# Mask products one step later, and a new order of loads, transposes and mask build, in a block-sparse attention with a feed-forward layer

## The chip, the cores and the metric

The kernel runs on one core of a Trainium2 chip. The metric is the device time of one execution in microseconds (us). An execution is called slow when it is more than 1.5% above the fastest of its kernel. Ratios and intervals leave those executions out; the quoted medians of four still contain them.

The engines: TensorE (PE) multiplies matrices, VectorE (DVE) and ScalarE (ACT) work element by element, GpSimd (POOL) does the same and issues most loads here, and SyncE (SP) issues the stores and the DMA transposes.

## The reference

Four batches, 8 heads, 768 positions, head size 64. A 768x768 mask in blocks of 32 says which keys a query sees. The attention output, as 3072 tokens of 512 values, goes through an RMS norm and a gated feed-forward layer.

```python
scores = scale * np.matmul(q, k.transpose(0, 1, 3, 2))
mask = ...                       # neighbours, first and last block, 3 sampled blocks per row
scores = np.where(mask, scores, -1e9)
attn = softmax(scores); attn_out = np.matmul(attn, v)
x = attn_out.transpose(0, 2, 1, 3).reshape(B * S, H * D)      # 3072 x 512
xn = x / sqrt(mean(x * x) + 1e-6) * rms_g
g = xn @ w_gate                                               # 512 -> 1536
out = (g * sigmoid(g) * (xn @ w_val)) @ w_out                 # 1536 -> 512
```

## The kernel before

The work is cut into 8 units: a unit `u` is one batch and one half of its queries (384 columns). Attention of a unit takes 12 steps: 4 head pairs `pr` with 3 steps each. A step computes two of the six key tiles `jt`: scores on TensorE (`qk_mm`), exp on ScalarE (`exp_`), mask product on VectorE (`mask_`). The sum over keys (`av`, `zsum`) and the normalisation (`norm_a` to `norm_e`) follow. The feed-forward (FF) items of the preceding units are fed in between by a credit scheme, so that TensorE has work while exp and mask run. The schedule is written out by hand: instructions stand in each engine's queue in the order in which the program emits them.

```python
def load_pair(b, pr):                       # q and k of one head pair: 4 loads
    ...                                     # tile layout (c, h, d) inside the pair
    for t, src in ((qraw[b], qv), (kraw[b], kv)):
        ...
        for h in range(2):
            nc.gpsimd.dma_start(out=dst[:, h], in_=sp[:, h])

def transposes_dma(b, pr):                  # 2 transposes per head pair
    x = qkpool.tile([P, 2, S], BF16, name="qkT", tag="qkT")
    for i, src in enumerate((qraw[b], kraw[b])):
        nc.sync.dma_start_transpose(
            out=x[:, i, :].rearrange("q (c p) -> q c p", c=NC),
            in_=src[:, 2 * pr:2 * pr + 2, :].rearrange("p h w -> p (h w)"))

def mask_build(ic):                         # one half of the mask, six evictions on VectorE
    qm = ...matmul...; nc.vector.tensor_copy(out=Qvis[:, cols], in_=qm)
    for jt in range(NC):
        mp = ...matmul...
        nc.vector.tensor_copy(out=Mk[:, jt, cols], in_=mp)

def av(n, shared):
    ...                                     # 12 matmuls into o_
    nc.scalar.copy(out=osb[u][:, pr, :], in_=o_)
    nc.gpsimd.tensor_tensor(                # the squares o2 for the norm
        out=o2s[u][:, pr, :], in0=osb[u][:, pr, :], in1=osb[u][:, pr, :], op=ALU.mult)

def norm_a(u): ...                          # zw += o2 (matmul), zs = copy of zw
def norm_b(u): ...; nc.gpsimd.tensor_tensor(out=rs, in0=ms, in1=nhalf, op=ALU.pow)   # the power
def norm_c(u): ...; nc.vector.tensor_tensor(out=fx, in0=rz, in1=rs..., op=ALU.mult)

# FF item g:  gp = wg.T @ xn;  th = tanh(gp/2) on ScalarE;  uu = (th+1)*gp on VectorE
# FF item v:  vp = wv.T @ xn;  hp = uu * vp on VectorE
# FF item y:  yp += hp.T @ wo; copy on ScalarE, store

LAG = 8
for n in range(NU * NP):
    s1 = 3 * (n + 1)
    at(s1, 1.2, av, n, n >= 8); at(s1, 0.7, zsum, n)
    if pr == NP - 1: ...                    # norm_a at s1 + 1 ... norm_e at s1 + 5 and s1 + 7
at(2, 1.6, mask_build, 1)
for b in range(1, B):
    for pr in range(NP):
        at(3 * (8 * (b - 1) + pr) + 1, 0, load_pair, b, pr)
        at(3 * (8 * (b - 1) + pr + (3 if b == 1 else 2)) + 1, 0, transposes_dma, b, pr)
    at(3 * (8 * (b - 1) + (1 if b == 1 else 4)) + 1, 0, load_v, b)
at(4, 0, load_wo)
# FF of unit u starts at step 12 * (u + 1) + LAG

# one step
sa = qk_mm(n, 2 * j);      exp_(n, 2 * j, sa)
sb = qk_mm(n, 2 * j + 1)
if step == 0: ...                           # mask_build(0) here
else:
    if queue: since += feed()               # one FF item
    exp_(n, 2 * j + 1, sb)
    mask_(n, 2 * j); mask_(n, 2 * j + 1)    # behind the exp of their own step
... # then the fixed work of the step, then more FF items by credit
```

The softmax here doesn't subtract the row's maximum and nothing guards it: scores larger than these inputs give would overflow.

## Time and profile before

| | before |
|---|---|
| time, median of the first 3 runs | 394.03 us (391.96 to 394.90) |
| span of the profiled run | 390.7 us |
| TensorE / VectorE / ScalarE busy | 85% / 64% / 57% |
| first FF matmul | 73.65 us |
| one unit in the steady state | 42.34 us |

The page's busy times, and its row of the granted TensorE clock in 40 slices of the span (tenths of full speed), of the kernel before:

```profile
PE 332.0 (85%) x2426; PEld 157.2 (40%) x2454; DVE 249.2 (64%) x527; ACT 222.1 (57%) x353; POOL 93.4 (24%) x130
...
PE   2687508798879999998989898999899899999995
...
PEclk9969756999989999999999999999999999999999
```

One slice is 9.8 us. The zero in the sixth place of the TensorE row belongs to a hole from 44.8 to 58.7 us. A caution on the clock row: its first nines are not a measurement. The trace's clock entries begin only at about 17 us here, and the time before them is counted as full speed; yet the 12 transposes of one tensor took 0.85 us at 15.03 us and 0.50 us at 27.11 us.

TensorE's waits, longest in total first (who waited for whom: total us, times, longest us):

```profile
PE zw L312 <- POOL o_324 L293: 13.9, 1, 13.9
PE vp L411 <- DVE hp L414: 5.4, 11, 0.9
...
PE mp L203 <- DVE Qvis L199: 2.6, 2, 2.0
```

The first line is the hole: one single wait of 13.9 us, in which the normalisation of unit 0 waits for a square (o2) on GpSimd. The timeline of GpSimd shows why it came late (start us, us, engine, line, operation, and in brackets the idle time before it and what ended that):

```profile
43.72 1.69 POOL L83 DMA_DIRECT2D qb<-in_q_dram  x2
47.33 0.82 POOL L83 DMA_DIRECT2D kb<-in_k_dram  x1 [1.92 <-DMA vb<-in_v_dram]
57.01 0.82 POOL L83 DMA_DIRECT2D kb<-in_k_dram  x1 [8.86 <-DMA wo<-in_moe_w_out_dram]
57.84 0.84 POOL L293 TENSOR_TENSOR o_324<-osb 128x384 bf16<-128x384 f32 x1
```

A load issue sat at the head of GpSimd's queue until the wo load had landed, and the square stood behind it. The chain of waits has the same story in three lines (start us, us, what):

```profile
37.72 19.00 DMA wo<-in_moe_w_out_dram
...
57.84 0.85 POOL o_324 L293
58.69 0.04 issue
58.73 0.48 PE zw L312
```

In the steady state, the busy times of one unit (window from one unit's power on GpSimd to the next: length, busy us of each engine, granted clock, DMA share, GB/s), and VectorE's waits in the same stretch:

```profile
221.23:263.57 42.34, 39.02 (x289) 18.46 (x293) 29.14 (x63) 27.55 (x45) 4.18 (x6) 1.00 0.10 29
```

```profile
DVE uu L400 <- ACT th L398: 6.1, 6, 2.7
DVE pt L268 <- ACT pt L262: 4.8, 5, 1.5
DVE hp L414 <- PE vp L411: 1.2, 3, 0.4
```

TensorE's waits in the same stretch:

```profile
PE vp L411 <- DVE hp L414: 1.1, 2, 0.9
PE yp L425 <- issue: 0.6, 4, 0.2
...
PE gp L394 <- DVE uu L400: 0.5, 1, 0.5
```

TensorE's records lack 3.3 us of being full. Of these, 0.6 us stand before yp matmuls where records are missing (the trace has 32 of the unit's 36), so some 2.7 us are really idle. VectorE is busy only 29.14 us, but for 4.8 us it stands before a mask product whose exp is not ready.

### The profile page before, as it was taken

To read this page: it belongs to the slowest core of one execution; us is meant where nothing else is said; L and a number is where in the kernel's file an instruction comes from. 1 tells how busy PE (TensorE), PEld (TensorE's weight loads), DVE (VectorE), ACT (ScalarE), POOL (GpSimd) and SP (SyncE) were. 2 spreads that over 40 slices of the span, in tenths; PEclk is the share of its full clock that TensorE was granted. 3 is DMA by queue.
4 is the path that set the end of the run, shared out by engine and by line. 5 is a ranking of instruction groups with operands and counts; after the bars stand their busy time and mean duration, and the time that the engine had idled before them with its cause. 6 is when DMAs were issued, how large, how long until landed. Compare 5 with 4: busy or idle time off the path is not lost.

```text
span 390.7 us, 6305 instructions
## 1 busy us (share of the span) xinstructions
PE 332.0 (85%) x2426; PEld 157.2 (40%) x2454; DVE 249.2 (64%) x527; ACT 222.1 (57%) x353; POOL 93.4 (24%) x130
## 2 busy tenths in 40 slices
PE   2687508798879999998989898999899899999995
PEld 1223103344334444444444443444444444555552
DVE  4866406767856776567765876667756777666550
ACT  1448406686747676676666566756667667333331
POOL 8934712115444110044334100001000101000000
PEclk9969756999989999999999999999999999999999
DMA  5999999008866930053999520000000000000012
GB/s 72 184 211 180 170 183 134 3 0 81 81 42 41 143 74 2 27 59 33 90 107 107 82 67 29 27 3 27 3 27 29 29 0 29 27 29 28 27 48 88
DMA packets 70850, 25.58 MB, mean 65 GB/s; under 512 B 58020, under 2 KB 67748, under 8 KB 70820
## 3 DMA queue, kind: packets, MB, share of 16 engines
q0 software_dynamic: 47600, 14.16, 35.0%
q1 hardware_dynamic: 23220, 11.02, 12.2%
q8 instruction: 19, 0.31, 0.3%
q14 instruction: 11, 0.09, 0.1%
HBM read 28.31 MB, written 6.29 MB: 89 GB/s over the span
## 4 chain that ended last, share of the span: by engine, by line
PE 50%; DVE 19%; ACT 11%; DMA 10%; issue 4%; POOL 4%; POOLq 0%; DVEq 0%; ACTq 0%
PE gp L394 10%; PE yp L425 10%; PE vp L411 9%; ACT pt L262 7%; DVE pt L268 7%; DMA wo<-in_moe_w_out_dram 5%; DMA wv<-in_moe_w_val_dram 5%; DVE uu L400 5%; PE zw L303 4%; ACT th L398 3%; DVE xn L379 3%; DVE hp L414 3%; PE oa L287 1%; PE vw L411 1%; PE gw L394 1%
## 5 line engine op out<-in xcount | busy, mean ns | idle before, releaser
L268 DVE TENSOR_TENSOR pt<-pt,Mk 128x768 bf16<-128x768 bf16 x192 | 101.9, 558 | 38.6 <-ACT pt L262 34.9
L400 DVE SCALAR_TENSOR_TENSOR uu<-th,gp 128x384 bf16<-128x384 bf16 x90 | 49.7, 552 | 50.2 <-ACT th L398 50.0
L411 PE MATMUL vp<-xn,wv 128*128 128x384 bf16 x360 | 74.0, 328 | 5.9 <-DVE hp L414 5.4
L394 PE MATMUL gp<-xn,wg 128*128 128x384 bf16 x360 | 73.9, 328 | 5.5 <-DVE uu L400 4.3
L398 ACT ACTIVATE th<-gp 128x384 bf16<-128x384 f32 x90 | 44.3, 492 | 52.9 <-PE gp L394 50.3
L425 PE MATMUL yp<-wo,hp 128*128 128x512 bf16 x260 | 70.8, 381 | 3.5 <-issue 3.1
L414 DVE TENSOR_TENSOR hp<-uu,vp 128x384 bf16<-128x384 bf16 x90 | 49.7, 552 | 14.1 <-PE vp L411 9.2
L394 PEld LDWEIGHTS <-wg 128*128 128x128 bf16 x384 | 35.6, 98 | 41.3 <-issue 16.7
L411 PEld LDWEIGHTS <-wv 128*128 128x128 bf16 x384 | 36.0, 99 | 35.3 <-issue 14.5
L255 PEld LDWEIGHTS <-qkT 64*128 64x128 bf16 x384 | 14.0, 95 | 65.4 <-issue 60.9
L425 PEld LDWEIGHTS <-hp 128*128 128x128 bf16 x288 | 26.2, 99 | 28.7 <-issue 7.5
L287 PEld LDWEIGHTS <-vb 128*64 128x64 bf16 x384 | 21.4, 114 | 18.0 <-issue 11.0
L83 POOL DMA_DIRECT2D kb<-in_k_dram x24 | 19.6, 819 | 16.3 <-DMA wo<-in_moe_w_out_dram 8.9
L431 ACT ACTIVATE yo<-yp 128x512 f32<-128x512 f32 x24 | 14.3, 597 | 15.3 <-PE yp L425 13.6
L303 PE MATMUL zw<-pt,Ez 128*32 128x384 bf16 x384 | 22.6, 344 | 0.0
L83 POOL DMA_DIRECT2D qb<-in_q_dram x24 | 20.5, 856 | 1.9 <-DMA wv<-in_moe_w_val_dram 1.9
L338 POOL TENSOR_TENSOR rs<-ms,nhalf 128x3 f32<-128x3 f32 x8 | 7.1, 887 | 44.4 <-DVE ms L335 44.4
L379 DVE SCALAR_TENSOR_TENSOR xn<-osb,gcol,fb 128x384 bf16<-128x384 f32 x28 | 15.9, 608 | 0.0
L312 PE MATMUL zw<-o_324,Ew 128*32 128x384 bf16 x4 | 0.8, 372 | 13.9 <-POOL o_324 L293 13.9
L303 PEld LDWEIGHTS <-Ez 128*32 128x32 bf16 x384 | 7.5, 98 | 12.6 <-issue 11.0
L316 DVE COPY zs<-zw 128x384 f32<-128x384 f32 x8 | 4.4, 551 | 12.7 <-PE zw L312 12.7
L287 PE MATMUL oa<-pt,vb 128*64 128x384 bf16 x96 | 12.2, 404 | 0.0
(558 smaller groups left out, 422.1 us busy)
## 6 DMA issues: line engine op xcount, KB each, us to landing
out_dram<-yo SPq DMA_DIRECT2D x24, 256.0 KB, 2.0
vb<-in_v_dram POOLq DMA_DIRECT2D x4, 768.0 KB, 8.1
qb<-in_q_dram POOLq DMA_DIRECT2D x24, 96.0 KB, 3.6
kb<-in_k_dram POOLq DMA_DIRECT2D x24, 96.0 KB, 3.7
wg<-in_moe_w_gate_dram POOLq DMA_DIRECT2D x2, 768.0 KB, 12.5
wv<-in_moe_w_val_dram POOLq DMA_DIRECT2D x2, 768.0 KB, 16.1
wo<-in_moe_w_out_dram POOLq DMA_DIRECT2D x1, 1536.0 KB, 19.0
qb<-in_q_dram POOLq DMA_DIRECT2D x2, 192.0 KB, 3.5
```

What stands on the lines that cost most here:

```text
L83: nc.gpsimd.dma_start(out=dst[:, h], in_=sp[:, h])
L262: nc.scalar.activation(out=ptiles[n][:, jt, :, :], in_=s_[:, :, 0:TG], func=AF.Exp, scale=SCALE)
L268: nc.vector.tensor_tensor(out=pv, in0=pv, in1=Mk[:, jt, ic * TG:(ic + 1) * TG].unsqueeze(1).to_broadcast([P, 2, TG]), op=ALU.mult)
L287: nc.tensor.matmul(out=o_[64 * e:64 * e + 64, :], lhsT=vb[:, 2 * pr + e, jt * D:(jt + 1) * D], rhs=pt_[:, jt, e, :], start=(jt == 0), stop ...
L303: nc.tensor.matmul(out=zwt[u][32 * c:32 * c + 32, :], lhsT=Ez[:, pr, :], rhs=pt_[:, 2 * j2 + par, e, :], start=(pr == 0 and j2 == 0), stop ...
L379: nc.vector.scalar_tensor_tensor(out=xns[u][:, pr, :], in0=osb[u][:, pr, :], scalar=gcol[:, pr:pr + 1], in1=fb[i], op0=ALU.mult, op1=ALU.mult)
L394: nc.tensor.matmul(out=gp, lhsT=wg[:, c, f * P:(f + 1) * P], rhs=xns[u][:, c, :], start=(c == 0), stop=(c == NP - 1))
L398: nc.scalar.activation(out=th, in_=gp, func=AF.Tanh, scale=0.5)
L400: nc.vector.scalar_tensor_tensor(out=uu, in0=th, scalar=1.0, in1=gp, op0=ALU.add, op1=ALU.mult)
L411: nc.tensor.matmul(out=vp, lhsT=wv[:, c, f * P:(f + 1) * P], rhs=xns[u][:, c, :], start=(c == 0), stop=(c == NP - 1))
L414: nc.vector.tensor_tensor(out=hps[u][:, f, :], in0=uu, in1=vp, op=ALU.mult)
L425: nc.tensor.matmul(out=yp, lhsT=hps[u][:, f, t * P:(t + 1) * P], rhs=wo[:, f, :], start=(f == 0), stop=(f == NF - 1))
```

## The change

Its intent: give VectorE mask products whose exp has long been done, take the first normalisation off GpSimd's load queue, put batch 1's loads in an order in which nothing needed soon stands behind a large load, make one DMA transpose per tensor and batch, build the mask in pieces and start the FF of unit 0 a step earlier.

```diff
-    def load_pair(b, pr): ...
+    def load_c(b, i, c):                     # rows (c, head, d): one load per tensor and c
+        nc.gpsimd.dma_start(
+            out=flat[:, c * DM:(c + 1) * DM].rearrange("p (h d) -> p h d", h=H),
+            in_=src[b, :, :, c * D:(c + 1) * D])
...
-    def transposes_dma(b, pr): ...           # 2 per head pair
+    def transposes_dma(b, i):
+        nc.sync.dma_start_transpose(
+            out=qk[b][:, i].rearrange("q c r p -> q (c r) p"),
+            in_=(qraw, kraw)[i][b].rearrange("p h w -> p (h w)"))
...
-        nc.gpsimd.tensor_tensor(
+        (nc.vector if u == 0 else nc.gpsimd).tensor_tensor(
             out=o2s[u][:, pr, :], in0=osb[u][:, pr, :], in1=osb[u][:, pr, :], op=ALU.mult)
...
-    LAG = 8
+    LAG = 9
-        at(s1, 1.2, av, n, n >= 8)
-        at(s1, 0.7, zsum, n)
+        at(s1 + 1, 1.25, av, n, n >= 8)
+        at(s1 + 1, 0.7, zsum, n)
... # normalisation one step later; unit 0's second half of norm_e at s1 + 6
-    at(2, 1.6, mask_build, 1)
+    at(1, 0.3, mask_query, 0); at(1, 0.3, mask_build, 0, 0, 4); at(2, 0.3, mask_build, 0, 4, 6)
+    at(5, 0.3, mask_query, 1)
+    for i in range(3):
+        at(6 + i, 0.3, mask_build, 1, 2 * i, 2 * i + 2)
...
+                at(base + (7 + c if b == 1 else 1 + 2 * c + i), 0, load_c, b, i, c)
+            at(base + 17, 0, transposes_dma, b, i)
-    at(4, 0, load_wo)
+    at(13, 0, load_wo)
...
-    START = UST + LAG
+    starts = [UST + 7] + [UST * (u + 1) + LAG for u in range(1, NU + 1)]
...
+                for m in late:
+                    mask_(*m)                # the two products of the step before
+                late = [(n, 2 * j), (n, 2 * j + 1)]
                 if queue:
                     since += feed()
                 exp_(n, 2 * j + 1, sb)
-                mask_(n, 2 * j)
-                mask_(n, 2 * j + 1)
```

(Cut: the layout of the transposed tile, TensorE's transposes of batch 0 with one copy on ScalarE, and one load each for wg and wv in place of two.)

More of the change, by code (lines that the diff above doesn't have):

```diff
@@ L49 @@
     vpool = ctx.enter_context(tc.tile_pool(name="vpool", bufs=2))
-    qkpool = ctx.enter_context(tc.tile_pool(name="qkpool", bufs=8))
+    qkpool = ctx.enter_context(tc.tile_pool(name="qkpool", bufs=2))
     ppool = ctx.enter_context(tc.tile_pool(name="ppool", bufs=2))
@@ L71, in load_qk @@
         nc.gpsimd.dma_start(out=kraw[b][:, lo:hi, :], in_=kv[b, :, lo:hi, :])
-    def load_pair(b, pr):
-        if b not in qraw:
-            qraw[b] = raw.tile([P, H, NC * D], BF16, name="qb", tag="qb")
-            kraw[b] = raw.tile([P, H, NC * D], BF16, name="kb", tag="kb")
-        for t, src in ((qraw[b], qv), (kraw[b], kv)):
-            dst = t[:, 2 * pr:2 * pr + 2, :].rearrange("p h w -> p (h w)").rearrange(
-                "p (c h d) -> p h c d", c=NC, h=2)
-            sp = src[b, :, 2 * pr:2 * pr + 2, :].rearrange("p h (c d) -> p h c d", c=NC)
-            for h in range(2):
-                nc.gpsimd.dma_start(out=dst[:, h], in_=sp[:, h])
+    def load_c(b, i, c):
+        src, t = ((qv, qraw), (kv, kraw))[i]
+        if b not in t:
+            t[b] = raw.tile([P, H, NC * D], BF16, name="qb", tag=("qb", "kb")[i])
+        flat = t[b].rearrange("p h w -> p (h w)")
+        nc.gpsimd.dma_start(
+            out=flat[:, c * DM:(c + 1) * DM].rearrange("p (h d) -> p h d", h=H),
+            in_=src[b, :, :, c * D:(c + 1) * D])
     def load_v(b):
@@ L137, with load_w @@
     wvv = moe_w_val.rearrange("(c p) f -> p c f", p=P)
-    FH = DFF // 2
-    def load_w(i):
-        nc.gpsimd.dma_start(out=wg[:, :, i * FH:(i + 1) * FH], in_=wgv[:, :, i * FH:(i + 1) * FH])
-        nc.gpsimd.dma_start(out=wv[:, :, i * FH:(i + 1) * FH], in_=wvv[:, :, i * FH:(i + 1) * FH])
+    def load_w():
+        nc.gpsimd.dma_start(out=wg, in_=wgv)
+        nc.gpsimd.dma_start(out=wv, in_=wvv)
     def load_wo():
@@ L159, with transposes @@
     qk = {}
-    def transposes(b, pr, early=False):
-        x = qkpool.tile([P, 2, S], BF16, name="qkT", tag="qkT")
-        qk[(b, pr)] = x
-        if early:
-            tt = [ps_f.tile([P, 1024], BF16, name="tq", tag="gp"),
-                  ps_f.tile([P, 1024], BF16, name="tk", tag="vp")]
-        else:
-            t_ = ps_s.tile([P, 2, 1024], BF16, name="tqk", tag="s")
-            tt = [t_[:, 0, :], t_[:, 1, :]]
+    def transposes(b, pr):
+        if b not in qk:
+            qk[b] = qkpool.tile([P, 2, NC, NP, P], BF16, name="qkT", tag="qkT")
+        x = qk[b][:, :, :, pr, :]
+        tt = [ps_f.tile([P, 1024], BF16, name="tq", tag="gp"),
+              ps_f.tile([P, 1024], BF16, name="tk", tag="vp")]
         for i, src in enumerate((qraw[b], kraw[b])):
@@ L175, in transposes, with mask_query @@
                         in_=src[:, 2 * pr + h, c * D:(c + 1) * D], identity=ident)
-        if early:
-            for i in range(2):
-                nc.vector.tensor_copy(out=x[:, i, :], in_=tt[i][:, 0:S])
-        else:
-            nc.vector.tensor_copy(out=x, in_=t_[:, :, 0:S])
-    def transposes_dma(b, pr):
-        x = qkpool.tile([P, 2, S], BF16, name="qkT", tag="qkT")
-        qk[(b, pr)] = x
-        for i, src in enumerate((qraw[b], kraw[b])):
-            nc.sync.dma_start_transpose(
-                out=x[:, i, :].rearrange("q (c p) -> q c p", c=NC),
-                in_=src[:, 2 * pr:2 * pr + 2, :].rearrange("p h w -> p (h w)"))
+        for i in range(2):
+            (nc.scalar.copy if i == 1 and pr == 0 else nc.vector.tensor_copy)(
+                out=x[:, i], in_=tt[i][:, 0:S].rearrange("q (c p) -> q c p", c=NC))
+    def transposes_dma(b, i):
+        if b not in qk:
+            qk[b] = qkpool.tile([P, 2, NC, NP, P], BF16, name="qkT", tag="qkT")
+        nc.sync.dma_start_transpose(
+            out=qk[b][:, i].rearrange("q c r p -> q (c r) p"),
+            in_=(qraw, kraw)[i][b].rearrange("p h w -> p (h w)"))
     Qvis = const.tile([32, S], BF16, name="Qvis")
     Mk = const.tile([P, NC, S], BF16, name="Mk")
-    def mask_build(ic):
+    def mask_query(ic):
         cols = slice(ic * TG, (ic + 1) * TG)
-        qm = ps_a.tile([32, TG], FP32, name="qm", tag="zw")
+        qm = ps_a.tile([32, TG], FP32, name="qm", tag="acc")
         nc.tensor.matmul(
@@ L199, in mask_build @@
         nc.vector.tensor_copy(out=Qvis[:, cols], in_=qm)
-        for jt in range(NC):
+    def mask_build(ic, lo, hi):
+        cols = slice(ic * TG, (ic + 1) * TG)
+        for jt in range(lo, hi):
             mp = (ps_a.tile([P, TG], FP32, name="mp", tag="acc") if jt % 2
@@ L241 @@
     nc.gpsimd.memset(nhalf, -0.5)
-    load_w(0)
-    load_w(1)
+    load_w()
     ptiles, osb, zwt, xns, hps, o2s = {}, {}, {}, {}, {}, {}
@@ L252, in qk_mm @@
         s_ = ps_s.tile([P, 2, 512], FP32, name="s_", tag="s")
-        x = qk[(b, pr)]
+        x = qk[b]
         for e in range(2):
@@ L256, in qk_mm @@
                 out=s_[:, e, 0:TG],
-                lhsT=x[64 * e:64 * e + 64, 1, jt * P:(jt + 1) * P],
-                rhs=x[64 * e:64 * e + 64, 0, ic * TG:(ic + 1) * TG], start=True, stop=True)
+                lhsT=x[64 * e:64 * e + 64, 1, jt, pr, :],
+                rhs=x[64 * e:64 * e + 64, 0, ic * NT:(ic + 1) * NT, pr, :],
+                start=True, stop=True)
         return s_
@@ L447 @@
         s1 = 3 * (n + 1)
-        at(s1, 1.2, av, n, n >= 8)
-        at(s1, 0.7, zsum, n)
+        at(s1 + 1, 1.25, av, n, n >= 8)
+        at(s1 + 1, 0.7, zsum, n)
         if pr == NP - 1:
-            at(s1 + 1, 0.4, norm_a, u)
-            at(s1 + 2, 0.5, norm_b, u)
-            at(s1 + 3, 0.0, norm_c, u)
-            at(s1 + 4, 0.3, norm_d, u)
-            at(s1 + 5, 0.35, norm_e, u, 0)
-            at(s1 + 7, 0.35, norm_e, u, 1)
-    for pr in range(1, NP):
-        at(3 * (pr - 1) + 1, 0.95, transposes, 0, pr, True)
-    at(2, 1.6, mask_build, 1)
-    for b in range(1, B):
-        for pr in range(NP):
-            at(3 * (8 * (b - 1) + pr) + 1, 0, load_pair, b, pr)
-            at(3 * (8 * (b - 1) + pr + (3 if b == 1 else 2)) + 1, 0, transposes_dma, b, pr)
-        at(3 * (8 * (b - 1) + (1 if b == 1 else 4)) + 1, 0, load_v, b)
-    at(4, 0, load_wo)
+            when = (2, 3, 4, 5, 6, 6) if u == 0 else (2, 3, 4, 5, 6, 8)
+            at(s1 + when[0], 0.4, norm_a, u)
+            at(s1 + when[1], 0.6, norm_b, u)
+            at(s1 + when[2], 0.0, norm_c, u)
+            at(s1 + when[3], 0.3, norm_d, u)
+            at(s1 + when[4], 0.35, norm_e, u, 0)
+            at(s1 + when[5], 0.35, norm_e, u, 1)
+    for pr in range(1, NP):
+        at(3 * (pr - 1) + 1, 0.95, transposes, 0, pr)
+    at(1, 0.3, mask_query, 0)
+    at(1, 0.3, mask_build, 0, 0, 4)
+    at(2, 0.3, mask_build, 0, 4, 6)
+    at(5, 0.3, mask_query, 1)
+    for i in range(3):
+        at(6 + i, 0.3, mask_build, 1, 2 * i, 2 * i + 2)
+    for b in range(1, B):
+        base = 24 * (b - 1)
+        for c in range(NC):
+            for i in range(2):
+                at(base + (7 + c if b == 1 else 1 + 2 * c + i), 0, load_c, b, i, c)
+        for i in range(2):
+            at(base + 17, 0, transposes_dma, b, i)
+        at(3 * (8 * (b - 1) + (4 if b == 1 else 5)) + 1, 0, load_v, b)
+    at(13, 0, load_wo)
     ffq = []
@@ L480 @@
     QKT = 0.52
-    START = UST + LAG
+    starts = [UST + 7] + [UST * (u + 1) + LAG for u in range(1, NU + 1)]
     rate = {}
     for u in range(NU):
-        lo = START + UST * u
+        lo, hi = starts[u], starts[u + 1]
         need = sum(i[0] for i in ffq[u])
-        for st in range(lo, lo + UST):
+        for st in range(lo, hi):
             need += sum(f[0] for f in fixed.get(st, ())) + (QKT if st < NSTEP else 0)
-        rate[u] = need / UST
-    step, credit = 0, 0.0
+        rate[u] = need / (hi - lo)
+    step, credit, u = 0, 0.0, -1
+    late = []
     queue = []
@@ L498 @@
     while True:
-        u, r = divmod(step - START, UST)
-        if u >= 0 and r == 0 and u < len(ffq):
+        if step in starts:
+            u = starts.index(step)
             queue += ffq[u]
@@ L510 @@
             sb = qk_mm(n, 2 * j + 1)
-            if step == 0:
-                exp_(n, 1, sb)
-                mask_build(0)
-                mask_(n, 0)
-                mask_(n, 1)
-            else:
+            if step < 2:
+                exp_(n, 2 * j + 1, sb)
+                late += [(n, 2 * j), (n, 2 * j + 1)]
+            else:
+                for m in late:
+                    mask_(*m)
+                late = [(n, 2 * j), (n, 2 * j + 1)]
                 if queue:
@@ L519 @@
                 exp_(n, 2 * j + 1, sb)
-                mask_(n, 2 * j)
-                mask_(n, 2 * j + 1)
             credit -= QKT
+        else:
+            for m in late:
+                mask_(*m)
+            late = []
         if todo:
```

## The prediction

> **What bounds the kernel now.** The page: TensorE busy 85% of 390.7 us, VectorE 64%, ScalarE 57%. Three regimes:
>
> 1. Start. The feed-forward (FF) matmuls, which later keep TensorE full, start only at 73.65 us (timeline). TensorE's waits list one of 13.9 us: zw waits for the square o2 of the first normalisation, on GpSimd. The chain of waits shows why: at 47.3 GpSimd's queue reaches a load issue that waits until the 1.5 MB wo load lands (19.0 us), and squares only at 57.84. Each load issue waits for the landing of the one eight before it (kb at 57.01 for wo, at 47.33 for vb, at 35.96 for wv). That nothing passes in GpSimd's queue is also in the Trainium skill ("Perfetto Trace Analysis", tensor engine instruction: GpSimd is strict FIFO); the trace agrees. The mask build sits as lumps of 6 evictions (3.27 us) in VectorE's queue.
> 2. First FF unit, 73.7 to 112: about 30 us of TensorE work (12x8 matmuls at 0.162 us, plus attention) in 38.5 us.
> 3. Steady state: 42.35 us a unit, TensorE busy 39.0 (windows). Of the 3.3 us idle, waits name 2 to 3: hp/uu late 1.6, xn late 0.9. VectorE has 29.2 us of work, but waits 4.8 us per unit for exp at the head of its queue (mask products), with FF products behind. The last 37 us are TensorE alone.
>
> **What the change does.**
> - Squares of unit 0 go to VectorE (4 x about 0.5 us); batch 1's loads come two per step from step 7, wo at step 13 after them. No square waits for wo: -13.9 us. The next GpSimd work, the power in norm_b at step 15, needs load 6 of batch 1 landed: estimated 43 us (wv landed at 35.67, then 6 x 1024 packets at the 1.1 ns of the 35 to 47 us stretch), about when it is needed. At most 1 to 2 us lost.
> - Mask build in pieces, FF a step earlier, 14 steps for the first unit: -3 us at the start, -3 us in the first FF unit.
> - Masks one step later: their inputs are ready, so VectorE's 4.8 us wait goes. TensorE gains at most 3.3 us a unit; I take 1.6, times 6: -10 us.
> - 16 load issues per batch become 12 (0.82 us each, off the path); packets stay the same. 24 transposes become 6, four times as long (1.22 us of issue become about 5). Batch 1's run beside the wo load, where issues took 4.5 to 5.3 us; estimated landing 62 to 70, needed at step 24, about 70: +1.
> - A mask ahead of the first FF product costs nothing while VectorE is 69% busy.
>
> Sum: 394.0 - 13.9 - 3 - 3 - 10 + 1 = about 365 us.
>
> **Prediction: 365 us, 8 in 10 between 355 and 375.** Faster by over 2%: 0.96; within 2%: 0.03; slower: 0.01.
>
> **What would show it.** The 13.9 us wait gone; first FF matmul at 54 to 58 us; mask products' wait for exp (34.9 us in all) under 10; unit period 40 to 41.5 us, TensorE busy over 95% of it; last phase unchanged near 37 us; batch 1's transposes landed by 70 us.
>
> **What would make it wrong.** Batch 1's transposes or loads late, so that step 24 stalls (370 or more). The period staying at 42.3 because TensorE's work sets it (about 374). Waits for ScalarE's exp in place of VectorE. Or a gapless TensorE, 39.5 us a unit (about 355).

## The result

The kernel after takes 363.55 us (median of 4, 361.84 to 366.58), the kernel before in the same job 393.14 us (median of 4). The ratio is 0.9252, 95% interval 0.9177 to 0.9328. Ratios here are the mean time of one kernel's fast runs over that of the other's of the same rounds, so they are not quite the ratio of the medians quoted. All outputs are right.

The same parts of the page, of the kernel after:

```profile
PE 333.8 (92%) x2454; PEld 159.1 (44%) x2454; DVE 246.9 (68%) x531; ACT 222.6 (61%) x354; POOL 84.5 (23%) x112
...
PE   2787789899799999999999999999999999999995
...
PEclk9998988999999999999999999999999999999999
```

TensorE's work is what it was (332.0 and 333.8 us busy; 28 yp records are missing in the first trace, with 3.1 us of gaps where they should be); the span lost idle time. The hole is gone. GpSimd's timeline at the place where the hole was:

```profile
28.95 0.88 POOL L79 DMA_DIRECT2D qb<-in_q_dram  x1 [7.51 <-DMA wg<-in_moe_w_gate_dram]
36.32 0.88 POOL L79 DMA_DIRECT2D qb<-in_k_dram  x1 [6.49 <-DMA wv<-in_moe_w_val_dram]
...
41.39 0.88 POOL L85 DMA_DIRECT2D vb<-in_v_dram  x1
42.26 1.03 POOL L142 DMA_DIRECT2D wo<-in_moe_w_out_dram  x1
48.27 1.05 POOL L332 TENSOR_TENSOR rs<-ms,nhalf 128x3 f32<-128x3 f32 x1 [4.99 <-DVE ms L329]
```

Load issues still wait here (7.51 us for wg, 6.49 us for wv), but while nobody needs GpSimd. All are through at 43.3 us, and the power of the first normalisation waits for its own input, not for a load. TensorE's timeline has the first FF matmul here:

```profile
54.94 1.46 PE L388 MATMUL gp<-xn,wg 128*128 128x384 bf16 x4
```

The steady state, one unit and VectorE's waits in it:

```profile
199.36:239.35 39.99, 39.33 (x295) 18.87 (x295) 28.79 (x63) 27.59 (x44) 5.92 (x6) 1.00 0.41 80
```

```profile
DVE uu L394 <- ACT th L392: 9.0, 10, 2.0
DVE xn L373 <- PE fb L368: 1.3, 1, 1.3
```

No mask product waits any more. VectorE is still idle, now before uu, for want of work. TensorE is busy 39.33 of 39.99 us (98%). Over the whole run the group of the mask products had 38.6 us of idle time before it (34.9 us of that for exp), and now:

```profile
L262 DVE TENSOR_TENSOR pt<-pt,Mk 128x768 bf16<-128x768 bf16 x192 | 101.1, 571 | 0.4
```

Where the 28.2 us of the two profiled spans went, by the start of each unit's power on GpSimd (an operation that both kernels have once a unit):

| stretch | before | after | difference |
|---|---|---|---|
| start to power of unit 0 | 63.26 | 48.27 | -15.0 |
| unit 0 to 1 | 31.93 | 33.43 | +1.5 |
| unit 1 to 2 | 42.28 | 38.26 | -4.0 |
| unit 2 to 6 (four periods) | 168.45 | 159.38 | -9.1 |
| unit 6 to 7 | 35.84 | 34.12 | -1.7 |
| unit 7 to the end | 48.94 | 49.04 | +0.1 |

The power stands one step later in the program after (step 15 for unit 0, before it was 14), so the first stretch holds a little more work there. And the clock differs in the start: in the stretches 20 to 40 and 40 to 60 us the granted clock was 0.83 and 0.60 in the kernel before, 0.91 and 0.83 after. How much of the first 15.0 us is clock was not separated. From the power of unit 2 to that of unit 6 it was 1.00 in both.

### The profile page after: what moved, and what is told of

Read it like the earlier page. It is cut to its first block, busy times and chain, and to the rows that moved or that the text cites. A ratio compares the mean times of both kernels' runs of the same rounds, so it can differ in the third digit from the quotient of the medians.

```text
span 362.5 us, 6294 instructions
## 1 busy us (share of the span) xinstructions
PE 333.8 (92%) x2454; PEld 159.1 (44%) x2454; DVE 246.9 (68%) x531; ACT 222.6 (61%) x354; POOL 84.5 (23%) x112
## 4 chain that ended last, share of the span: by engine, by line
PE 75%; ACT 11%; DVE 7%; issue 4%; DMA 1%; POOL 1%; POOLq 0%; ACTq 0%; DVEq 0%
PE yp L419 16%; PE gp L388 15%; PE vp L405 12%; ACT pt L256 6%; PE zw L297 5%; PE oa L281 3%; ACT th L392 3%; DVE uu L394 2%; DVE pt L262 1%; PE zt L317 1%; DMA kb<-in_k_dram 1%; PE fb L368 1%; DVE xn L373 1%; PE vw L405 1%; PE gw L388 1%
## 5 line engine op out<-in xcount | busy, mean ns | idle before, releaser
L419 PE MATMUL yp<-wo,hp 128*128 128x512 bf16 x288 | 76.1, 380 | 0.0
L248 PEld LDWEIGHTS <-qkT 64*128 64x128 bf16 x384 | 13.9, 94 | 47.1 <-issue 45.5
L281 PEld LDWEIGHTS <-vb 128*64 128x64 bf16 x384 | 24.5, 115 | 16.8 <-issue 11.1
L425 ACT ACTIVATE yo<-yp 128x512 f32<-128x512 f32 x24 | 14.3, 597 | 13.6 <-PE yp L419 12.1
L79 POOL DMA_DIRECT2D qb<-in_q_dram x18 | 16.4, 909 | 7.7 <-DMA wg<-in_moe_w_gate_dram 7.5
L79 POOL DMA_DIRECT2D qb<-in_k_dram x18 | 16.2, 901 | 7.1 <-DMA wv<-in_moe_w_val_dram 6.5
L281 PE MATMUL oa<-pt,vb 128*64 128x384 bf16 x96 | 12.6, 413 | 0.2 <-DVE Mk L199 0.2
L287 POOL TENSOR_TENSOR o_3107<-osb 128x384 bf16<-128x384 f32 x4 | 4.1, 1032 | 29.2 <-ACT osb L286 29.2
L287 POOL TENSOR_TENSOR o_2595<-osb 128x384 bf16<-128x384 f32 x4 | 4.1, 1030 | 28.3 <-ACT osb L286 28.3
## 6 DMA issues: line engine op xcount, KB each, us to landing
wg<-in_moe_w_gate_dram POOLq DMA_DIRECT2D x1, 1536.0 KB, 14.1
```

Source lines behind the costliest of these rows:

```text
L79: nc.gpsimd.dma_start(out=flat[:, c * DM:(c + 1) * DM].rearrange("p (h d) -> p h d", h=H), in_=src[b, :, :, c * D:(c + 1) * D])
L281: nc.tensor.matmul(out=o_[64 * e:64 * e + 64, :], lhsT=vb[:, 2 * pr + e, jt * D:(jt + 1) * D], rhs=pt_[:, jt, e, :], start=(jt == 0), stop ...
L419: nc.tensor.matmul(out=yp, lhsT=hps[u][:, f, t * P:(t + 1) * P], rhs=wo[:, f, :], start=(f == 0), stop=(f == NF - 1))
```

## The experiments

The open question was not the size of the gain but which parts make it. Two readings of the hole stood against each other. Theory A, which the prediction's wording leans on: the square is what hangs on GpSimd, so moving it frees the start. Theory B: the order of the loads is the cause; whatever stands next on GpSimd hangs. For the steady state: is it the mask delay, or the extra step before av and the normalisation, or fewer load issues and transposes?

### One part alone, on the kernel before: b_sq and b_wo

```diff
 b_sq
-        nc.gpsimd.tensor_tensor(
+        (nc.vector if u == 0 else nc.gpsimd).tensor_tensor(
 b_wo
-    at(4, 0, load_wo)
+    at(13, 0, load_wo)
```

> The kernel before, with only the squares of unit 0 moved to VectorE. Theory A (as the prediction put it: the square is what waits on GpSimd, so its move takes away the 13.9 us): 379 to 381 us. Theory B (the same blocked load issue also stands ahead of the power in norm_b, step 15, so the wait only moves from TensorE's zw to VectorE's fx): the power still starts at about 58 us, a gain of about 5 us, 386 to 390 us.

> The kernel before, with only the wo load moved from step 4 to step 13, after batch 1's loads. If the order of the loads in GpSimd's queue is the cause (theory B), no load issue waits for wo while unit 0 needs GpSimd, the 13.9 us wait falls under 2 us and the time is 379 to 382 us. If the move of the squares is needed (theory A), the square still comes late and the gain is under 5 us.

b_sq: 387.44 us, ratio 0.986 (0.983 to 0.990). b_wo: 382.19 us, ratio 0.976 (0.970 to 0.981). Moving the squares gave 5 us, not 14. GpSimd's timeline of b_sq, and VectorE's wait:

```profile
57.56 0.82 POOL L83 DMA_DIRECT2D kb<-in_k_dram  x1 [9.13 <-DMA wo<-in_moe_w_out_dram]
58.39 0.91 POOL L338 TENSOR_TENSOR rs<-ms,nhalf 128x3 f32<-128x3 f32 x1
```

```profile
DVE fx L344 <- POOL rs L338: 10.6, 1, 10.6
```

The same blocked issue now holds the power instead of the square, and the wait has moved from TensorE to VectorE. On the kernel before, theory A falls and B stands. b_wo, which leaves the squares on GpSimd, took out 10 us. It did not reach the "under 2 us" that was expected for the rest, as TensorE's waits in b_wo show:

```profile
PE zw L312 <- POOL o L293: 4.0, 1, 4.0
```

Its last load issue of batch 1 (46.60 us) waited for v to land, and the square came at 47.44:

```profile
46.60 0.82 POOL L83 DMA_DIRECT2D kb<-in_k_dram  x1 [1.48 <-DMA vb<-in_v_dram]
47.44 0.84 POOL L293 TENSOR_TENSOR o<-osb 128x384 bf16<-128x384 f32 x1
```

### One part taken back, from the kernel after: a_sqpool, a_wo4, and both

```diff
 a_sqpool
-        (nc.vector if u == 0 else nc.gpsimd).tensor_tensor(
+        nc.gpsimd.tensor_tensor(
 a_wo4
-    at(13, 0, load_wo)
+    at(4, 0, load_wo)
 a_wo4_sq: both
```

> The kernel after, with unit 0's squares back on GpSimd. Theory B: batch 1's loads are all issued by 41.4 us, the last square is wanted at 43.6 us, so nothing is lost: ratio to before as that of after (0.925), 363 to 365 us. Theory A: the wait of zw for o2 returns, at least 3 us more than after, 367 or more.

> The kernel after, with only the wo load back at step 4, ahead of batch 1's loads. Theory B: from the eighth load of batch 1 on, issues wait for wo's landing, at about 45 us, and the power of norm_b (48.3 us in after) comes after about 50 us; batch 1's data and its transposes land some 9 us later: 3 to 8 us more than after (367 to 372). If moving the squares alone freed unit 0 (theory A): within 1 us of after, 363 to 365.

> The kernel after with both wo at step 4 and unit 0's squares on GpSimd; each alone cost at most 1.5 us. Theory C (the two are insurances for each other: with wo early, GpSimd reaches its next work only after the last issue of batch 1, at about 49.5 us, and the last square, wanted at 43.6, would come then): the wait of zw for o2 is back with about 5 us, 367 to 371 us. If load order and squares are both without weight in this schedule: within 2 us of after.

a_sqpool: 363.30 us (ratio 0.928), no different from after. a_wo4: 364.77 us (ratio 0.930, 0.925 to 0.934), about 1 us more, which the spread of the runs does not show; 3 to 8 had been expected. It lies where theory A had put it, within 1 us of after: in this schedule, unlike that of b_sq, moving the squares is enough even with wo early. Both together: 368.64 us (ratio 0.938, 0.934 to 0.942). The wait is back, in TensorE's waits and GpSimd's timeline of a_wo4_sq:

```profile
PE zw L306 <- POOL o L287: 5.7, 1, 5.7
```

```profile
43.63 0.87 POOL L79 DMA_DIRECT2D qb<-in_k_dram  x1 [4.66 <-DMA wo<-in_moe_w_out_dram]
...
47.80 0.88 POOL L79 DMA_DIRECT2D qb<-in_k_dram  x1
48.69 0.84 POOL L287 TENSOR_TENSOR o<-osb 128x384 bf16<-128x384 f32 x1
```

So each of the two measures is an insurance for the other in this schedule. The trace of a_wo4 shows two reasons why its expectation missed. The power came at 49.47 instead of 48.27 us, and VectorE waited 1.8 us for it, not more. And although batch 1's data landed later, its two transposes, which ran after wo had landed, were quicker. SyncE's timeline, a_wo4 first, then after:

```profile
53.41 9.23 SPq L177 DMA_TRANSPOSE qkT<-qb  x2
```

```profile
45.84 18.31 SPq L177 DMA_TRANSPOSE qkT<-qb  x2
```

They were issued by 62.6 us in one kernel and by 64.2 us in the other: what beside wo takes 18.31 us takes 9.23 without it. The Trainium skill ("DMA: Bandwidth & Descriptors", Queues, rings and completion order) says that each DMA engine goes round the queues that have work for it, packet by packet; the two durations agree with two queues sharing the engines.

### The mask delay: a_mask_now and b_mask_late

```diff
 a_mask_now (from after)
                 exp_(n, 2 * j + 1, sb)
+                if step > 2:
+                    for m in late:
+                        mask_(*m)
+                    late = []
 b_mask_late (from before)
+                for m in late:
+                    mask_(*m)
+                late = [(n, 2 * j), (n, 2 * j + 1)]
                 if queue:
                     since += feed()
                 exp_(n, 2 * j + 1, sb)
-                mask_(n, 2 * j)
-                mask_(n, 2 * j + 1)
 ... # and av, zsum and the normalisation one step later, LAG = 9
```

> The kernel after, with the mask products from step 3 on again behind the exp of their own step; av, normalisation and start steps stay as in after. If the mask delay is what shortened the unit from 42.35 to 39.99 us: the unit returns to about 42 us, VectorE waits again 4 to 5 us per unit for exp, and the time is 12 to 15 us more than after, 375 to 379. If the later av and normalisation (one step more of slack) did it: the unit stays near 40 us and the time within 2 us of after.

> The kernel before, with only the mask products one step later in VectorE's queue and what that needs (av, zsum and the normalisation one step later, LAG 9). If the mask delay is what works in the steady state: unit near 40 us, gain of 12 to 15 us there, 378 to 382 us, while the 13.9 us wait for o2 stays. If it only works together with the other parts: unit over 41.5 us, gain under 5 us.

a_mask_now: 384.72 us (ratio 0.976, 0.969 to 0.983). b_mask_late: 378.98 us (ratio 0.964, 0.959 to 0.970). A unit of a_mask_now, and VectorE's waits in it:

```profile
213.77:256.60 42.83, 39.20 (x289) 18.64 (x293) 29.32 (x63) 27.68 (x45) 5.09 (x6) 1.00 0.40 74
```

```profile
DVE uu L394 <- ACT th L392: 5.7, 6, 2.3
DVE pt L262 <- ACT pt L256: 5.4, 6, 1.5
DVE hp L408 <- PE vp L405: 1.2, 3, 0.4
```

The unit is back at 42.8 us with the extra step before av and the normalisation still in place. So it is the place of the mask products in VectorE's queue, not the slack around av, that shortens the unit. In b_mask_late the unit is 40.18 us (212.97 to 253.15 us) and the first FF matmul stays at 73.42 us, because the wait for o2 sets the start there. The Trainium skill ("Perfetto Trace Analysis", Tensor Engine Instruction) says of VectorE's queue what it says of GpSimd's: strict FIFO. This pair agrees: 5.4 us of waiting per unit, and 2.8 us of a unit's time, depend on order alone.

a_mask_now cost 21 us where 12 to 15 had been expected. By the powers on GpSimd, 14.1 us of it lie between units 1 and 7 (245.86 against 231.76 us), the mechanism that was meant. The other 7 us lie before unit 1's power. There the granted TensorE clock was lower as well (0.74 and 0.73 in the two stretches 20 to 40 and 40 to 60 us, against 0.91 and 0.83 in after). How much of the 7 us is order and how much is clock, these runs do not tell.

### Do the two add up: b_wo_mask

The edit is that of b_wo and that of b_mask_late.

> The kernel before with two of the parts only: wo issued at step 13 and the mask products one step later. Alone they gave ratios 0.976 and 0.964. If they add up: ratio about 0.94, 368 to 370 us, and what is left to the kernel after (0.925) is the start (mask pieces, first unit from step 19). If they overlap: 372 us or more. If the mask delay also frees the start once the wo wait is gone: 366 or less.

368.45 us, ratio 0.9385 (0.931 to 0.946). The product of the two single ratios is 0.976 x 0.964 = 0.941. They add up. About 1.3% (5 us) of the change is left for everything else; the interval of after, 0.918 to 0.933, just touches that of b_wo_mask.

### The rest: a_pairdma and a_masklump

```diff
 a_pairdma (from after): load_pair as before, at base + 7 + pr (b = 1) or base + 1 + 3 * pr
+        for i, src in enumerate((qraw[b], kraw[b])):
+            nc.sync.dma_start_transpose(
+                out=qk[b][:, i, :, pr, :],
+                in_=src[:, 2 * pr:2 * pr + 2, :].rearrange("p h w -> p (h w)"))
 a_masklump (from after)
-    at(1, 0.3, mask_build, 0, 0, 4)
-    at(2, 0.3, mask_build, 0, 4, 6)
-    at(5, 0.3, mask_query, 1)
-    for i in range(3): at(6 + i, 0.3, mask_build, 1, 2 * i, 2 * i + 2)
+    at(1, 0.3, mask_build, 0, 0, 6)
+    at(2, 0.3, mask_query, 1)
+    at(2, 0.3, mask_build, 1, 0, 6)
```

> The kernel after, with the loads of q and k by head pairs again (16 per batch) and 24 DMA transposes in place of 6, at the same steps. If the new layout of loads and transposes is worth nothing by itself (my view: same packets, off the critical path): within 1% of after, 361 to 367 us, unit 40 us. The rival, that fewer issues on GpSimd or fewer transposes carry part of the gain: 3 us or more over after, seen before 70 us in the timeline.

> The kernel after, with the mask build in two lumps of six evictions at steps 1 and 2. If the pieces matter as predicted (about 3 us at the start): the first feed-forward matmul at 57 to 58 us in place of 54.9 and 2 to 3 us more than after. If the start is paced by other things: within 1 us of after.

a_pairdma: 363.90 us, ratio 0.9258 against 0.9252 of after, first FF matmul at 54.78 us. 16 load issues instead of 12 and 24 transposes instead of 6 make no difference. a_masklump: 369.68 us, ratio 0.935 (0.927 to 0.943), 1.1% or about 4 us over after by the means, with intervals that overlap; the first FF matmul came at 61.69 us, with a granted clock of 0.75 from 40 to 60 us (0.83 in after). The four executions ran from 364.69 us (mean clock 0.993) to 371.30 us (0.975, called slow), so the size of this part is known only to a few us, and that it is there at all is likely but not clear of the noise.

### An attempt to beat it: a_start and a_start3

In the start of the kernel after, ScalarE is idle 4.6 us before one exp, because the scores stand behind transposes and mask matmuls on TensorE. a_start begins the mask at step 0 and spreads the rest; a_start3 mends the waits that its trace showed. (Added lines only; those that they replace are left out.)

```diff
+        at(s1 + (2 if u == 0 else 1), 0.7, zsum, n)
+    at(0, 0.3, mask_query, 0); at(0, 0.3, mask_build, 0, 0, 2); at(1, 0.3, mask_build, 0, 2, 4)
+    for pr, st in ((1, 1), (2, 3), (3, 6)):          # a_start3: (2, 5)
+        at(st, 0.95, transposes, 0, pr)
+    at(1, 0.3, mask_build, 0, 4, 6)
+    at(6, 0.3, mask_query, 1)                        # a_start3: step 5
+    for i, st in enumerate((8, 9, 11)):              # a_start3: (8, 8, 11)
+        at(st, 0.3, mask_build, 1, 2 * i, 2 * i + 2)
```

> An attempt to beat the kernel after, in the start only: the mask build of the first half begins at step 0, ahead of the transposes of pair 1, and zsum, transposes and the second half of the mask are spread so that no step holds av, zsum and transposes together. ScalarE sat idle 4.6, 2.1 and 2.7 us before exp in these steps. If those idle times set the start: first feed-forward matmul at 50 to 52 us in place of 54.9, 2 to 5 us less than after, 358 to 361. If the throttled TensorE clock or VectorE's work sets it: within 1 us of after.

> The attempt at the start, corrected by its trace: there TensorE waited 1.25 and 1.09 us for the data of pair 2 (transposed too early, at step 3) and 1.1 us for a mask eviction that held av's accumulator. Pair 2's transposes go to step 5, the second half of the mask to steps 8, 8 and 11, never just before an av. If these waits set the start: first feed-forward matmul at 51 to 52.5 us and 1 to 3 us less than the first attempt, 359 to 361. If the normalisation chain and the granted clock set it: 53 to 54 us again, and no difference from the first attempt that the spread of the runs would show.

a_start: 361.93 us, ratio 0.920 (0.915 to 0.925). a_start3: 362.41 us in five rounds, ratio 0.922 (0.919 to 0.925). Both intervals overlap with that of after (0.918 to 0.933), and the first FF matmul came at 53.78 and 54.15 us instead of the 50 to 52.5 that was expected. A gain over the kernel after is possible but not shown; if there is one, it is about half a per cent. Whether ScalarE's idle times set the start was not really tested, because most of them only moved: its listed waits before an exp, up to the first FF matmul, add up to 12.6 us in after, 11.8 in a_start and 11.4 in a_start3. Taking out TensorE's waits for pair 2 (1.25 and 1.09 us in a_start) in a_start3 brought no gain that the runs show. What sets the start, the runs leave open: the profiled run of a_start3, its slowest (365.87 us), had a granted clock of 0.78 and 0.71 in the two stretches from 20 to 60 us, where after had 0.91 and 0.83.

## Why the prediction was right

The time was predicted at 365 us and came out at 363.55. Point by point:

- **"No square waits for wo: -13.9 us."** The 13.9 us wait is gone, and the power of unit 0 comes 15.0 us earlier. The prediction names both measures, the squares' place and wo's, and does not say which does it. The experiments show that the cause is what stands ahead of unit 0's work in GpSimd's queue: moving the squares alone gave 5 us, moving wo alone 10 us, and in the schedule after either measure is enough (363.30 and 364.77 us), while without both the wait is back (368.64 us).
- **The power "about when it is needed", at most 1 to 2 us lost.** GpSimd was free at 43.3 us (estimated 43) and the power's input came at 48.27. Nothing was lost. That the estimate hit so closely is partly luck: its time per packet is not in the trace. From 35 to 47 us the kernel before moved 7363 packets, 1.6 ns each; the kernel after moved 9644 from 35 to 43 us, 0.83 ns each.
- **First FF matmul at 54 to 58 us.** It came at 54.94.
- **"-3 us at the start, -3 us in the first FF unit."** The first FF matmul came 18.7 us earlier, against 13.9 + 3 in the sum. From the power of unit 0 to that of unit 2 it was 1.5 - 4.0 = -2.5 us. The second -3 did not show as such: from the first FF matmul to the power of unit 2 the kernel before took 63.82 us, the kernel after 65.02 (with two steps more in it). The lumped mask alone cost about 4 us, not clear of the noise. The longer first unit and its earlier start were not tried alone, nor were the copy on ScalarE and the single loads of wg and wv.
- **Steady state: "I take 1.6, times 6: -10 us."** The mechanism was right, and shown in both directions. The size per unit was too small: 2.35 us (42.34 to 39.99), where half of 3.3 us had been taken. It is 70% of that figure, and nearly 90% of the 2.7 us that were really idle. The unit came out at the lower edge of the stated 40 to 41.5 us. The four full periods gave 9.1 us. VectorE's wait for exp went from 34.9 us to at most 0.4; under 10 had been said. TensorE is busy 98% of a unit; over 95% had been said.
- **Transposes of batch 1 "landing 62 to 70", +1 us.** The second was issued by 64.2 us, and TensorE never waits for it. The +1 was not needed. That fewer load issues are "off the path" is confirmed by a_pairdma.
- **The last phase unchanged.** From the last unit's power to the end: 48.94 and 49.04 us.

That the sum came so close is partly luck, since the terms missed in both directions. Up to the power of unit 2 the profiled spans differ by 17.5 us, where 13.9 + 3 + 3 = 19.9 had been taken (and the kernel after is one step further there); over the next five units by 10.8 us, where 10 had been taken; at the end by 0.1 us the other way; and the transposes cost nothing instead of 1. In all -28.2 us against -28.9. The prediction also started from 394.0 us, while the kernel before took 393.14 us in the job of the result.

## What to carry to other kernels

Read an in-order queue by what stands at its head: work that is ready behind something that is not ready costs as much as work that is not ready, and moving the waiting instruction alone can hand the wait to the next one behind the same head (10.6 us of it in b_sq). Emit a product one step after the result that it needs, if the buffers allow it; here it was worth 13.6 us on the kernel before (with av and the normalisation moved along) and, taken back alone, 21 us on the kernel after (7 of them in the start, where the clock differed too), while each engine's work stayed what it was. When several measures guard against the same wait, take each back alone and then together before calling one of them the cause.

## What the Trainium skill lacked or had wrong

- No page has this: on GpSimd's load queue an issue was held until the load eight issues before it had landed. kb at 57.01 us waited 8.86 us for wo, kb at 47.33 for vb, and in the kernel after the issues at 28.95 and 36.32 us waited 7.5 and 6.49 us for wg and wv, each eight issues back. Whether the chip or the software that places the semaphores sets this number, the runs do not tell.
- "TensorE: Matmul & The Clock Gate", HAM oscillation, gives "no PE-idle gaps >~3.4µs" as the rule for keeping the clock. It was not enough here. In the kernel before the granted clock was 0.52 in the stretch from 20 to 25 us, where TensorE's records are busy 4.68 of 5.00 us; its longest listed wait from the first score matmul to there was 2.0 us (for Qvis). A later part of the same page (A second HAM failure mode) does tell of a clock lost to short idle times between groups of matmuls, so the rule is incomplete rather than unknown to the page. The page (Part 1) says that the default is throttled and activity releases it, and that the ramp costs under 1% of a typical span. In the unit windows shown here from the steady state the granted clock was 1.00, which agrees. But the four executions of the kernel after, 361.84, 362.86, 364.23 and 366.58 us, had mean clocks of 0.990, 0.984, 0.985 and 0.971, and their times spread by 1.3%. In the profiled one (0.985) the recorded slow stretches lie between 27 and 58 us, but for the last microsecond; the other three were not profiled. Before the first clock entry, at about 24 us, this trace too counts full speed, while the 12 matmuls of one av took 2.13 us at 19.71 us and 1.17 us in the steady state. So the slow part of the start is longer than the mean clocks say, and it limits what can be shown about the start.
- "DMA: Bandwidth & Descriptors" has no figure for DMA transposes beside loads: the same two transposes took 18.31 us of issue beside the wo load and 9.23 us without it.
